# Attention and a Fourier mixer on one TensorE: another order for short matmul steps and pieces of VectorE work

## Chip, cores, metric

One core of one Trainium2 chip. The metric is the device time of one execution in microseconds (us). Times are medians. TensorE is called PE in the profiles, VectorE DVE, ScalarE ACT, GpSimd POOL; SP only issues transfers. L405 is line 405 of the kernel that was profiled, so the same statement has slightly different numbers in the kernel before, the changed kernel and the experiments.

## The reference

Block-sparse attention for four batches and eight heads (768 rows, head width 64) feeds a Fourier mixer with a feed-forward part. Cut to what matters:

```python
# q, k, v: (4, 8, 768, 64) float32; mask: blocks of 32, window, border blocks, three random ones
scores = np.where(mask, scale * q @ k.T, -1e9)
attn = softmax(scores) @ v                         # (4, 8, 768, 64)
x = attn.transpose(0, 2, 1, 3).reshape(4, 768, 512)

u = x + np.real(fft(fft(x, axis=1), axis=2))       # Fourier mixing
un = (u - mean(u)) / sqrt(var(u) + 1e-6)
out = u + np.maximum(un @ w_ch1, 0) @ w_ch2        # 512 -> 2048 -> 512, weights given as float64
```

The float64 weights come in as 32-bit words and are rounded to float32 on the chip.

## The kernel before

The kernel works through 96 attention steps, 24 to a batch and six to a pair of heads. A step makes two units of scores `s`, their exponentials and the product with the mask `e` (ScalarE, VectorE), and one step later the values `o`. Beside the attention of batch b it works off the mixer of batch b-1. Its front is a chain: divide by the sums and fold the symmetric halves (VectorE, into `sa`, `sd`), the two transforms (`zp`, then `pq`), normalization, turning the result (`utp`). Behind the front stand the channel steps: 32 of `hp` (eight matmuls each) and 24 of `y` (eight each), which need nothing but weights and the turned rows and fill most of the time.

Besides these there are short pieces, three or four small matmuls with a copy behind them: the turn of q and k of the next pair (`tp`), the place of a finished attention output into `x` (`xt`), the total of a pair's sums (`sp`). All of them share one buffer in PSUM, where a matmul's result lies until an engine copies it out: the pool `ps_t`. A piece can start only when the copy of the piece before it has emptied the buffer.

```python
ps_t = ctx.enter_context(tc.tile_pool(name="ps_t", bufs=1, space=PSUM))
...
def turn(n):                                  # q and k of a pair, all in one go
    raw = loaded.pop(n)
    for a, t in enumerate(raw):
        for half in range(2):
            tp = ps_t.tile([P, HS], FP32, tag="t", name="tp")
            for c in range(T):
                nc.tensor.transpose(tp[:, c * P:(c + 1) * P], t[:, T * half + c, :, :], ident)
            if half == 0:
                nc.vector.tensor_copy(out=dst[:, 0:HS], in_=tp)
            else:
                nc.scalar.copy(out=dst[:, HS:S], in_=tp)
        ...
def place(n, half):
    ...
    nc.vector.tensor_copy(out=x_of[b, half][:, :, j * P:(j + 1) * P], in_=xt)
...
def fill():                                   # mixer steps, paid from a budget per attention step
    spent = 0.0
    while early and spent < RATE / 2 and len(late) <= 4 * T:    # front: fold, zp, pq, utp
        cost, fn = early.popleft(); fn(); spent += cost
    ...
    while spent < RATE and late:                                # channel steps
        cost, fn = late.popleft(); fn(); spent += cost

def slot(sl):
    ...values and scores of the step...
    if 0 < sl <= B * SB and sl % (SP // 2) == 0:
        ...
        place(n, half)
    if sl > SB and sl % SP == 0 and sl <= B * SB:
        total(sl // SP - 1)
    if sl >= SB + 2 and (sl - 2) % SB == 0 and (sl - 2) // SB <= B:
        norm(b); queue.append(mixer(b, ...))
    if sl % SP == 3 and sl // SP + 1 < len(pairs):
        turn(n); load_qk(n + 1)
    ...
    fill()
```

The rounding of a weight chunk ends with a product and a sum on GpSimd. The first pair's q and k are loaded on one queue, q first.

Of the kernel before, what the change touches and what calls it, by code (L numbers as in the profile page):

```python
# [82 lines left out]
def kernel(  # L83
# [84 lines left out]
    def load_q(dst, b, h, n):  # L168

        for t in range(C):  # L170
            if t < T:
                for p0, cnt, rows in _rows(q[b, h], t, ((S * D, n),)):
                    nc.sync.dma_start(out=dst[p0:p0 + cnt, t, 0:n, :], in_=rows)
                continue
            for i in range(n):
                for p0, cnt, rows in _rows(q[b, h + i], t):
                    nc.sync.dma_start(out=dst[p0:p0 + cnt, t, i, :], in_=rows)

    def load_qk(n):

        b, j = pairs[n]
        qt = ld.tile([P, C, 2, D], FP32, tag="q", name="qr")
        load_q(qt, b, 2 * j, 2)
        kt = ld.tile([P, C, 2, D], FP32, tag="k", name="kr")
        for i in range(2):
            nc.sync.dma_start(out=kt[:, :, i, :],
                              in_=k[b, 2 * j + i].rearrange("(p c) d -> p c d", p=P))
        loaded[n] = (qt, kt)
# [83 lines left out]
    def mask_step(c):  # L272

        for half in range(2):
            m = ps_m.tile([P, 512], FP32, tag="m", name="m")
            nc.tensor.matmul(m[:, 0:HS], of_k[0:NB, c * P:(c + 1) * P],
                             keep_q[0:NB, half * HS:(half + 1) * HS], start=True, stop=True)
            nc.scalar.copy(out=mask[:, c, half * HS:(half + 1) * HS], in_=m[:, 0:HS])
# [59 lines left out]
    for w, w_sb in ((w_ch1, w1_sb), (w_ch2, w2_sb)):  # L338
        rows, cols = w.shape
        words = _words(w, rows * cols)  # L340
        for col in range(0, cols, WN):
            for row in range(rows // P):
                src = bass.AP(tensor=words, offset=2 * (row * P * cols + col),
                              ap=[[2 * cols, P], [1, 2 * WN]])
                wchunks.append((src, w_sb[:, row, col:col + WN]))
# [12 lines left out]
    def w_load(i):  # L358

        n1 = len(wchunks) // 2  # L360
        t = room(2 + i % 4 if i < n1 else 4 + i % 2, [P, 3 * WN], "wraw", U32)
# [3 lines left out]
    def w_round(i):  # L365
# [16 lines left out]
        nc.gpsimd.tensor_mul(out=a.bitcast(FP32), in0=lo.bitcast(FP32), in1=a.bitcast(FP32))  # L382
        nc.gpsimd.tensor_add(out=dst, in0=dst, in1=a.bitcast(FP32))
# [8 lines left out]
    def turn(n):  # L392

        raw = loaded.pop(n)
        out2 = []
        for a, t in enumerate(raw):
            dst = tp_p.tile([P, S], FP32, tag="qk"[a] + "T", name="qk"[a] + "T")
            for half in range(2):
                tp = ps_t.tile([P, HS], FP32, tag="t", name="tp")
                for c in range(T):  # L400
                    nc.tensor.transpose(tp[:, c * P:(c + 1) * P],  # L401
                                        t[:, T * half + c, :, :], ident)
                if half == 0:
                    nc.vector.tensor_copy(out=dst[:, 0:HS], in_=tp)  # L404
                else:  # L405
                    nc.scalar.copy(out=dst[:, HS:S], in_=tp)
# [3 lines left out]
            out2.append(dst)  # L410
        turned[n] = out2
# [5 lines left out]
    def scores(u):  # L417
        n, w = divmod(u, UP)
        half, c = divmod(w, C)
        qT, kT = turned[n]  # L420
# [30 lines left out]
    def values(u):  # L451
# [10 lines left out]
        if c == C - 1:  # L462
            if half == 1:
                v_of.pop(n)
                turned.pop(n)
# [4 lines left out]
    def place(n, half):  # L470
# [5 lines left out]
        xt = ps_t.tile([P, T, P], FP32, tag="t", name="xt")  # L476
        for c in range(T):
            nc.tensor.transpose(xt[:, c, :], oT[:, c * P:(c + 1) * P], ident)
        nc.vector.tensor_copy(out=x_of[b, half][:, :, j * P:(j + 1) * P], in_=xt)  # L479
# [40 lines left out]
    def norm(b):  # L520

        r = sm.tile([P, T, 4, NP], FP32, tag="r", name="r", bufs=2)
        for half in range(2 if b == 0 else 1):
# [5 lines left out]
            if b > 0:  # L529
                nc.vector.reciprocal(out=r, in_=st[:, :, :, 0:NP])  # L530
                continue
# [4 lines left out]
        if b == 0:  # L536
            nc.vector.reciprocal(out=r, in_=r)
        for half in range(2):
            for c in range(T):
                xc = x_of[b, half][:, c, :].rearrange("p (j i d) -> p j i d", i=2, d=D)  # L540
                rc = r[:, c, 2 * half:2 * half + 2, :].rearrange("p i (j o) -> p j i o", o=1)
                nc.vector.tensor_tensor(out=xc, in0=xc, in1=rc.broadcast_to([P, NP, 2, D]),  # L542
                                        op=ALU.mult)
# [6 lines left out]
    def fourier(b, xA, xB, uns):  # L550
# [3 lines left out]
        def fold():  # L554
            sa = next_room([P, T, DM], "sa")
            sd = next_room([P, T, DM], "sd")
            e1 = un_p.tile([P, DM], FP32, tag="un", name="e1")
            tt = nc.vector.tensor_tensor
            tt(out=sa, in0=xA, in1=xB, op=ALU.add)
            tt(out=sd, in0=xA, in1=xB, op=ALU.subtract)  # L560
            tt(out=sa[:, :, 1:M], in0=sa[:, :, 1:M], in1=_run2(sa, DM - 1, M - 1, -1), op=ALU.add)
            tt(out=sd[:, :, 1:M], in0=sd[:, :, 1:M], in1=_run2(sd, DM - 1, M - 1, -1),
               op=ALU.subtract)

            b1 = xB[:, 1, :]
# [4 lines left out]
            top = slice(DM - QD, DM)  # L570
            for f in (sa, e1.rearrange("p (o d) -> p o d", o=1)):
                tt(out=f[:, :, top], in0=f[:, :, 0:QD], in1=_run2(f, M, QD, -1), op=ALU.add)  # L572
                tt(out=f[:, :, 0:QD], in0=f[:, :, 0:QD], in1=_run2(f, M, QD, -1),
                   op=ALU.subtract)

            tt(out=sd[:, :, top], in0=sd[:, :, 0:QD], in1=_run2(sd, M, QD, -1), op=ALU.subtract)
            tt(out=sd[:, :, 1:QD], in0=sd[:, :, 1:QD], in1=_run2(sd, M - 1, QD - 1, -1),
               op=ALU.add)
            nc.vector.tensor_copy(out=sd[:, :, 0:1], in_=sd[:, :, QD:QD + 1])
            st["f"] = (sa, sd, e1)  # L580
            st["z"] = tr_p.tile([P, 4, KS], FP32, tag="tr", name="z")
            st["side"] = sm.tile([1, KS], FP32, tag="side", name="side", bufs=1)
# [3 lines left out]
        def along(g):  # L586

            sa, sd, e1 = st["f"]
            ps = ps_m.tile([P, 512], FP32, tag="m", name="zp")
# [28 lines left out]
        def across(m):  # L618
# [18 lines left out]
            tt = nc.vector.tensor_tensor  # L637
# [36 lines left out]

        steps = [(0.0, fold)]
        steps += [(2.0, lambda g=g: along(g)) for g in range(5)]
        for m in range(T):
            def both(m=m):
                across(m)
                whiten(0, m)  # L680
            steps.append((1.2, both))
        return steps, whiten
# [3 lines left out]
    def mixer(b, xA, xB):  # L686

        uns, unT = {}, {}
        first, whiten = fourier(b, xA, xB, uns)
# [12 lines left out]
        def hidden(half, f):  # L702
            if f % 4 == 0:
                if b == half == f == 0:

                    turns[0] = ROOMS
# [30 lines left out]
        first += [(0.6, lambda m=m: un_flip(0, m)) for m in range(T)]  # L737
        rest = []
        for half in range(2):
            for f in range(NF):  # L740
                rest.append((2.6, lambda half=half, f=f: hidden(half, f)))
                if half == 0 and f in (2, 4, 6):
                    rest.append((0.0, lambda m=f // 2 - 1: whiten(1, m)))
                if half == 0 and f in (5, 7, 9):
                    rest.append((0.6, lambda m=(f - 5) // 2: un_flip(1, m)))
            for m in range(T):
                for part in range(4):
                    rest.append((3.5, lambda half=half, m=m, p=part: channels(half, m, p)))
        return first, rest

    def run_all(steps):
        for _, fn in steps:
            fn()
# [3 lines left out]
    RATE = 5.6  # L757
    W_PACE = 0.9
    SP = UP // SLOT
    SB = SP * NP  # L760
    early, late, queue = deque(), deque(), deque()
    w_next = w_got = 0

    def fill():


        if not early and queue and queue[0][0]:
            early.extend(queue[0][0])
            queue[0][0].clear()
        spent = 0.0  # L770
        while early and spent < RATE / 2 and len(late) <= 4 * T:
            cost, fn = early.popleft()
            fn()
            spent += cost
        if not early and queue and not queue[0][0]:
            late.extend(queue.popleft()[1])
        while spent < RATE and late:
            cost, fn = late.popleft()
            fn()
            spent += cost  # L780

    def slot(sl):
        nonlocal w_next
        units = range(SLOT * sl, SLOT * sl + SLOT)
        if 0 < sl <= B * SB:
# [3 lines left out]
            if sl <= SB:  # L789
# [3 lines left out]
        if sl < B * SB:  # L793
            for u, s in [(u, scores(u)) for u in units]:
                weigh(u, s)
        if 0 < sl <= B * SB and sl % (SP // 2) == 0:
            n, half = divmod(sl // (SP // 2) - 1, 2)
            b, j = pairs[n]
            while j == 0 and b >= 2 and (b - 2, half) not in finished:
                late.popleft()[1]()  # L800
            place(n, half)
        if sl > SB and sl % SP == 0 and sl <= B * SB:
            total(sl // SP - 1)
        if sl >= SB + 2 and (sl - 2) % SB == 0 and (sl - 2) // SB <= B:
            b = (sl - 2) // SB - 1
            norm(b)
            queue.append(mixer(b, x_of.pop((b, 0)), x_of.pop((b, 1))))
# [141 lines left out]
```

## Time and profile before

| kernel before | |
|---|---|
| median of the first three runs | 1451.74 us (1449.76 to 1460.52) |
| span of the profiled run | 1454.3 us |
| PE busy, PE idle | 1224.2 us, 230.1 us |
| first scores, first hp | 18.99 us, 275.7 us |

PE is the bound, and its busy time includes the extra that a slow clock costs. So I take three numbers from every profile: PE idle (span less busy); PE's excess busy time over 1112 us, the prediction's estimate of the same matmuls at full clock; and whatever PE's view of waits names. The prediction shows the main lines.

```profile
618.23 7.94 DMA out_dram<-x
```

The copy that places attention output into `x` waits twice for an output transfer that still reads that buffer, for two batches earlier. Such a transfer takes 8 us. PE's two longest waits of `sp` for `x` in the prediction's list, 9.36 and 9.20 us of its 42.4, are this; the prediction overlooked it.

### The profile page before, as it was taken

Reading aid. Unit: us, or ns where it says so; the run is one execution under the profiler, and the core shown is the slowest. Engines: PE = TensorE matmul, PEld = TensorE weight load, DVE = VectorE, ACT = ScalarE, POOL = GpSimd, SP = SyncE. Lnnn points to the kernel's source line nnn. Section 1 sums busy time; section 2 is a strip of 40 time slices with the busy share of each in tenths; the row PEclk is TensorE's granted clock in tenths of the full one; section 3 lists DMA queues with packets and bytes.
Section 4 is the critical chain, followed back from the end, with each engine's and each line's share of the span. In section 5 each row is a group of like instructions: output and inputs, shape, how many; then the busy total and the mean of one; then the engine's idle time right before and its main releaser. Section 6 shows DMA issues by size and latency. Waiting matters only on the chain.

```text
span 1454.3 us, 11918 instructions
## 1 busy us (share of the span) xinstructions
PE 1224.2 (84%) x4412; PEld 574.2 (39%) x4412; DVE 426.2 (29%) x817; ACT 310.0 (21%) x541; POOL 321.6 (22%) x245
## 2 busy tenths in 40 slices
PE   5888748789898968868989895878999996899996
PEld 1222214344334423434434442334444443454552
DVE  2335184443122252413212225322221223320000
ACT  3455324232112112113112211202212110010000
POOL 1225253344222221112222221202222220000000
PEclk9899878799999989889999998889999998999998
DMA  4433321111010100000010000000100000000000
GB/s 117 114 110 99 91 69 51 40 32 45 17 38 8 26 7 22 8 18 22 11 37 19 22 11 8 22 25 1 33 8 8 8 1 8 8 7 8 15 2 23
DMA packets 65281, 44.26 MB, mean 30 GB/s; under 512 B 52902, under 2 KB 58048, under 8 KB 65216
## 3 DMA queue, kind: packets, MB, share of 16 engines
q1 hardware_dynamic: 65216, 43.42, 10.8%
q8 instruction: 37, 0.61, 0.2%
q14 instruction: 28, 0.23, 0.1%
HBM read 37.11 MB, written 6.29 MB: 30 GB/s over the span
## 4 chain that ended last, share of the span: by engine, by line
PE 67%; DVE 7%; ACT 2%; DMA 1%; issue 1%; DVEq 0%; ACTq 0%
PE y L725 24%; PE hp L710 23%; PE o L460 6%; PE s L423 6%; PE tp L401 2%; DVE e L443 2%; PE zp L596 1%; DMA out_dram<-x 1%; DVE x L542 1%; ACT s L441 1%; PE utp L697 1%; PE zp L607 1%; PE sp L516 1%; DVE x L479 1%; DVE kT L404 0%
## 5 line engine op out<-in xcount | busy, mean ns | idle before, releaser
L710 PE MATMUL hp<-unT,w_sb 128*128 128x384 f32 x1024 | 358.9, 508 | 2.0 <-ACT unT L698 2.0
L725 PE MATMUL y<-w_sb,hs 128*128 128x512 f32 x768 | 351.0, 612 | 0.0
L449 POOL TENSOR_TENSOR acc<-acc,e 128x768 f32<-128x768 f32 x96 | 175.2, 1825 | 404.1 <-DVE e L443 400.3
L710 PEld LDWEIGHTS hp<-unT,w_sb 128*128 128x128 f32 x1024 | 199.4, 199 | 150.9 <-issue 31.4
L443 DVE TENSOR_TENSOR e<-s,mask 128x768 f32<-128x768 f32 x144 | 131.1, 952 | 339.3 <-ACT s L441 339.3
L725 PEld LDWEIGHTS y<-w_sb,hs 128*128 128x128 f32 x768 | 148.5, 197 | 186.0 <-issue 182.8
L460 PE MATMUL o<-e,vr 128*64 128x384 f32 x768 | 159.0, 532 | 11.2 <-ACT e L439 8.4
L441 ACT ACTIVATE s<-s 128x768 f32<-128x768 f32 x144 | 108.0, 792 | 243.8 <-PE s L423 243.8
L423 PE MATMUL s<-qT,kT 64*128 64x384 f32 x768 | 159.6, 524 | 0.0
L716 DVE TENSOR_SCALAR hs<-hp 128x384 f32<-128x384 f32 x64 | 35.6, 557 | 220.7 <-PE hp L710 220.7
L423 PEld LDWEIGHTS s<-qT,kT 64*128 64x128 f32 x768 | 65.3, 189 | 84.8 <-issue 66.4
L714 ACT ACTIVATE hs<-hp 128x384 f32<-128x384 f32 x64 | 31.4, 491 | 314.0 <-PE hp L710 314.0
L447 POOL TENSOR_TENSOR acc<-e 128x768 f32<-128x768 f32 x24 | 43.3, 1806 | 228.7 <-PE sp L516 124.8
L460 PEld LDWEIGHTS o<-e,vr 128*64 128x64 f32 x768 | 47.7, 142 | 109.1 <-issue 82.7
L382 POOL TENSOR_TENSOR wraw<-wraw 128x512 f32<-128x512 f32 x32 | 41.5, 1297 | 192.4 <-issue 73.0
L596 PE MATMUL zp<-cs_sb,sa 128*128 128x385 f32 (+1 forms) x48 | 27.4, 712 | 53.4 <-DVE sa L572 53.4
L401 PE MATMUL tp<-ident,qr 128*128 128x128 f32 x96 | 24.8, 335 | 51.4 <-DVE x L479 28.7
L730 DVE TENSOR_TENSOR x<-y,x 128x512 f32<-128x512 f32 x24 | 16.6, 691 | 159.9 <-PE y L725 159.9
L439 ACT ACTIVATE e<-s 128x768 f32<-128x768 f32 x48 | 38.8, 811 | 55.1 <-PE s L428 55.1
L516 PE MATMUL sp<-acc,pick 128*32 128x384 f32 x96 | 13.1, 618 | 42.4 <-DVE x L479 42.4
L401 PE MATMUL tp<-ident,kr 128*128 128x128 f32 x96 | 27.6, 422 | 19.9 <-DVE kT L404 10.4
L375 DVE TENSOR_SCALAR wraw<-wraw 128x512 uint32<-128x512 uint32 x32 | 16.4, 512 | 93.8 <-ACT wraw L374 93.7
(139 smaller groups left out, 719.8 us busy)
## 6 DMA issues: line engine op xcount, KB each, us to landing
wraw<-in_moe_w_ch_dram SPq DMA_DIRECT2D x32, 512.0 KB
kr<-in_k_dram SPq DMA_DIRECT2D x32, 192.0 KB
vr<-in_v_dram SPq DMA_DIRECT2D x32, 192.0 KB
qr<-in_q_dram SPq DMA_DIRECT2D x128, 32.0 KB
out_dram<-x SPq DMA_DIRECT2D x16, 128.0 KB
out_dram<-x SPq DMA_DIRECT2D x8, 256.0 KB
qr<-in_q_dram SPq DMA_DIRECT2D x64, 31.5 KB
qr<-in_q_dram SPq DMA_DIRECT2D x64, 0.2 KB
```

What stands on the lines that cost most here:

```text
L382: nc.gpsimd.tensor_mul(out=a.bitcast(FP32), in0=lo.bitcast(FP32), in1=a.bitcast(FP32))
L401: nc.tensor.transpose(tp[:, c * P:(c + 1) * P], t[:, T * half + c, :, :], ident)
L423: nc.tensor.matmul(s[:, i, 0:HS], kT[D * i:D * i + D, c * P:(c + 1) * P], qT[D * i:D * i + D, half * HS:(half + 1) * HS], start=True, stop ...
L439: nc.scalar.activation(out=e, in_=s[:, :, 0:HS], func=ACT.Exp, scale=scale)
L441: nc.scalar.activation(out=s[:, :, 0:HS], in_=s[:, :, 0:HS], func=ACT.Exp, scale=scale)
L443: nc.vector.tensor_tensor(out=e, in0=s[:, :, 0:HS], in1=m.broadcast_to([P, 2, HS]), op=ALU.mult)
L447: nc.gpsimd.tensor_add(out=acc_of[n, half], in0=e_of[u - 1], in1=e)
L449: nc.gpsimd.tensor_add(out=acc_of[n, half], in0=acc_of[n, half], in1=e)
L460: nc.tensor.matmul(o[D * i:D * i + D, :], vt[:, i, c, :], e[:, i, :], start=(c == 0), stop=(c == C - 1))
L596: mm(ps[rows, 0:KS], sa[:, t, cols], cs_sb[:, t, :], start=(t == 0), stop=False)
L710: nc.tensor.matmul(ps[:, 0:T * P], w1_sb[:, d, f * P:(f + 1) * P], unT[half][:, d, :], start=(d == 0), stop=(d == ND - 1))
L725: nc.tensor.matmul(y, hs[half, f // 4][:, f % 4, m * P:(m + 1) * P], w2_sb[:, f, :], start=(f == 0), stop=(f == NF - 1))
```

## The change

Intent: put every short piece behind a channel step, one at a time, so that PE has long matmuls to run while the piece's copy empties the shared buffer; cut VectorE's long front work into eight folds and six scalings that go between channel steps as well; and keep channel steps of the last batch back (28, then 12) for the front of the next. With that go several smaller edits. The diff, cut to its core:

```diff
-    def turn(n):                       # four tp groups, one behind the other
+    def turn(n, a, half):              # one tp group; four calls per pair
+        pool, tag = small(pairs[max(n - 1, 0)][0])      # batch 0: ps_m (two buffers), else ps_t
...
-                if half == 0:
-                    nc.vector.tensor_copy(out=dst[:, 0:HS], in_=tp)
-                else:
-                    nc.scalar.copy(out=dst[:, HS:S], in_=tp)
+        if a == 0:
+            nc.vector.tensor_copy(out=dst[:, half * HS:(half + 1) * HS], in_=tp[:, 0:HS])
+        else:
+            nc.scalar.copy(out=dst[:, half * HS:(half + 1) * HS], in_=tp[:, 0:HS])
...  place:
-        nc.vector.tensor_copy(out=x_of[b, half][:, :, j * P:(j + 1) * P], in_=xt)
+        nc.scalar.copy(out=x_of[b, half][:, :, j * P:(j + 1) * P],
+                       in_=xt[:, 0:HS].rearrange("p (c f) -> p c f", c=T))
...  w_round:
-        nc.gpsimd.tensor_mul(out=a.bitcast(FP32), in0=lo.bitcast(FP32), in1=a.bitcast(FP32))
-        nc.gpsimd.tensor_add(out=dst, in0=dst, in1=a.bitcast(FP32))
+        nc.vector.tensor_mul(out=a.bitcast(FP32), in0=lo.bitcast(FP32), in1=a.bitcast(FP32))
+        nc.vector.tensor_add(out=dst, in0=dst, in1=a.bitcast(FP32))
...  load_qk:
+        second = nc.scalar if n == 0 else nc.sync       # first k and half of first q: ScalarE's queue
...
+    RATE = 2.4                          # channel steps per attention step
+    def gap():                          # behind every channel step
+        if short:
+            short.popleft()()           # one short piece, or
+            return
+        room_for = 2                    # up to two pieces of VectorE work or one group of front matmuls
+        while apart and room_for > 0:
+            kind, fn, need = apart[0]
+            if kind == "p" and room_for < 2:
+                return
+            while len(late) > need:     # need: channel steps kept back
+                channel_step()
+            apart.popleft()
+            ...
+    def begin(b):
+        hold = 4 * T
+        wide = hold + NF
+        steps = [(kind, fn, wide) for kind, fn in norm_steps(b) + first]
...  slot:
+            for at, a, half in ((1, 0, 0), (2, 0, 1), (4, 1, 0), (5, 1, 1)):
+                if s == at:
+                    short.append(lambda a=a, half=half: turn(n + 1, a, half))
...
+        state["owed"] = min(state["owed"] + RATE, RATE + 1) if late else 0.0
+        gap()
+        while late and state["owed"] >= 1:
+            channel_step()
+            state["owed"] -= 1
+            gap()
+        while short:
+            gap()
```

Also: six buffers for weight chunks in place of four and then two, 1.3 chunks per attention step in place of 0.9, and the chunks in another order; two mask matmuls per attention step as short pieces; the loads of q and k for a later pair at step 5 in place of 3; and the second half of a batch's first pair is placed two attention steps later.

## The prediction

> **What bounds the kernel now.** I read the page first: busy time by engine, then the 40 slices.
>
> ```profile
> PE 1224.2 (84%) x4412; PEld 574.2 (39%) x4412; DVE 426.2 (29%) x817; ACT 310.0 (21%) x541; POOL 321.6 (22%) x245
> ...
> PE   5888748789898968868989895878999996899996
> ...
> PEclk9899878799999989889999998889999998999998
> ```
>
> TensorE is the bound, 84% busy; nothing else passes 29%. The slices where PE falls to 4 to 6 are those where the clock falls to 7 or 8. They come about every 350 us: at the start of each batch's Fourier mixer. PE is idle for 1454 - 1224 = 230 us. The view of waits, PE alone, says why:
>
> ```profile
> PE zp L596 <- DVE sa L572: 53.4, 4, 14.5
> PE sp L516 <- DVE x L479: 42.4, 12, 9.4
> PE tp L401 <- DVE x L479: 28.7, 15, 3.4
> PE pq L614 <- DVE x L657: 13.7, 3, 4.6
> PE tp L401 <- DMA qr<-in_q_dram: 13.0, 6, 4.4
> ```
>
> All waits of PE in that view sum to 218 us; the other 12 are the output at the end. The three largest, 124 us, are of one kind: a short matmul stands in PE's order directly behind the VectorE piece or the PSUM buffer that it needs, with long matmuls behind it that could have run. The timeline of PE inside an otherwise full stage shows one:
>
> ```profile
> 700.03 0.55 PE L478 MATMUL xt<-ident,oT 128*128 128x128 f32 x3
> 702.83 0.85 PE L516 MATMUL sp<-acc,pick 128*32 128x384 f32 x8 [2.25 <-DVE x L479]
> 703.61 5.43 PE L710 MATMUL hp<-unT,w_sb 128*128 128x384 f32 x16
> ```
>
> sp needs the one buffer that xt filled; its copy waits in VectorE's queue behind two mask products (952 ns each). PE stands for 2.25 us with two hp steps ready behind it.
>
> **The floor.** I take each kind of matmul where the timeline shows it back to back at granted clock 1.00. Channel steps: the last stage has 128 hp in 41.28 us and 96 y in 41.20 us, so 322 and 429 ns; 1024 x 0.322 + 768 x 0.429 = 660 us. Attention: a step of two units takes 697.10 to 700.03 = 2.93 us for o and s; 96 of them 281. The first batch also has the mask as a matmul and its sums: 0.74 + 0.78 a step, x24 = 36. Short groups tp and xt: 96 groups of three x 0.48 = 46. Later sums 12 x 0.78 = 9, mask 3. The Fourier part (zp, pq, end, utp, st) by its start-to-start intervals is about 19 a batch, 76. Sum: **1112 us**. Busy time is 1224, so 112 us are the slow clock; idle 230. 1112 + 112 + 230 = 1454.
>
> **What the Trainium skill says.** "TensorE: Matmul & The Clock Gate", "HAM oscillation": the clock is full only while PE stays busy, and gaps longer than some 3.4 us put it to half. The trace agrees in kind and is harsher: after gaps of only 2 us, eight hp matmuls took 4.36 us instead of 2.58. The same page, Part 2: matmuls stay in program order, only weight loads are pulled ahead; so the place in PE's order decides, as the 2.25 us show. "Perfetto Trace Analysis", "Matmuls": independent groups should rotate through PSUM banks so that one's evacuation overlaps the next one's matmuls; xt, tp, sp share one buffer here, and the waits above are its price. "SBUF — State Buffer", "Who interferes with whom": VectorE reading two SBUF inputs contends with GpSimd. Agrees: the rounding's scalar_tensor_tensor took 0.69 us alone and 1.66 us beside GpSimd's product.
>
> **The change part by part.**
>
> 1. *One short piece behind each channel step.* No matmul is added or removed; the order on each engine changes, and I compared both orders. In the new one tp, xt, sp and st stand alone between hp or y steps of 2.58 or 3.43 us, which is longer than an evacuation (0.56 us) even behind two mask products (1.82). The fold and scaling (before: some 14 us of VectorE in one run, with PE waiting) are cut into pieces and, for batches 1 to 3, stand behind channel steps kept back for that. So sp<-x (42.4), tp<-x (28.7), tp<-qT/kT (28) and about 40 of the 53.4 us for zp should go: about 139 us.
>
> 2. *No filler for batch 0.* The first batch has no channel steps, and the new order has up to three gaps of short work per attention step instead. There the first hp comes three attention steps later than before. VectorE work in this stage: ten steps x 1.82 = 18, scaling 5, fold 12, pq and normalization 16, copies 4 = 55 us; PE's own work is about 29 + 19 + 5 = 53. With the chains s, exp, product, o in each step, I estimate 78 us, of them 25 idle. Before, the stretch from 187 to 276 us took 89 with fewer attention steps.
>
> 3. *Ends of the later fronts.* In batches 1 and 2 the order runs out of channel steps at pq; the last pq and the utp behind it stand with only attention steps of 2.93 us between. A pq piece is some 4.5 us of VectorE plus 2.4 of normalization. I keep 6 to 7 us idle a batch, 20 in all.
>
> 4. *q and k in four parts, first loads on two queues.* The six tp groups wait for qr 4.4, 1.4, 1.3, 2.0, 2.1, 1.9 us, since 18 q loads take 11 us to issue one after the other. k and half of q go to ScalarE's queue, which is idle then: first scores at about 14 us instead of 19.
>
> 5. *Rounding on VectorE alone, all six buffers, pace 1.3.* Removed: 64 GpSimd operations of 1.30 us, none of which PE waited for. Added to VectorE: 64 x about 0.59 (a 1536-wide fp32 sum takes 1.76) = 38 us. A chunk is then 0.46 + 0.72 + 0.40 + 1.18 = 2.76 us; at 1.3 a step 3.6 of the 4.84 us that a step of batch 0 takes. With tables and copies about 85% of VectorE: it fits. ScalarE: 1.62 of exp, 1.46 of rounding, 0.8 of copies = 3.9 of 4.84. Weights finish at step 25 instead of 36, and the deeper prefetch should remove the one stall of 6.7 us where o waited for an exp behind a late chunk. The mask matmuls come two a step with one free buffer: about 12 us idle where 4.7 were.
>
> **The sum.** Idle left: start 10, batch 0 20, first front 25, later fronts 20, scattered 15 (a pq holds one of the two channel buffers), output 12 = 102 us. Slow clock: before, 112 us for 230 idle, 0.49 each; 0.49 x 102 = 50. 1112 + 102 + 50 = **1264 us**, a ratio of 0.87.
>
> **Rivals.** (a) *VectorE takes over as the wait.* Its queue is first in, first out; two pieces behind one step (up to 3.5 us) plus the two products delay o and the copies that free PSUM. For: the first front holds 55 us of VectorE work in 78. Against: 29% busy overall, and o has waited only 11 us for e. If it bites in every front and in batch 0, +50: 1310. (b) *Transfers bound batch 0.* 16.8 MB of weights, 5.9 of q, k, v and 1.4 of tables in about 130 us is 186 GB/s; the most that a 30 us window moved is 156 GB/s at a busy share of 0.53, so room seems left, but packets of q are small and ScalarE's queue stops exp behind a late chunk. Worth +15 to +30. (c) *The clock stays full.* If gaps become too short to trip the gate, slow clock goes to 15 or less: 1220. (d) *Nothing moves,* because waits only shift to the next matmul in order. Against: the channel steps were runnable when PE stood idle, and no engine is near full; I give this little.
>
> **Range and chances.** (c) with small leftovers gives 1210, (a) and (b) together 1325. Even half of the recovered idle leaves about 1360, below the 2% line at 1423. Predicted 1264, 1210 to 1325; faster by over 2%: 0.96, within 2%: 0.03, slower: 0.01.
>
> **What would show it.** Right: sp<-x and tp<-x gone from PE's waits, zp's wait at most one long item (batch 0), mean granted clock near 0.95 to 0.96, PE busy near 1160 in a span of 1264, first hp before 240 us, all slices from the tenth on at 9 apart from one per batch. Wrong: o waiting for VectorE's e over 40 us in total (rival a), exp or rounding waiting for weight transfers over 15 us (rival b), the clock still at 0.91, or hp and y waiting for their own evacuations, which they never did before.

## More of the kernel before

One more pair belongs here, from the view of DVE's waits and from the chain of waits of the kernel before (columns of the first: us in total, times, longest; of the second: start, duration, what):

```profile
DVE x L479 <- DMA out_dram<-x: 16.4, 2, 8.3
```

## The result and the profile after

| | before | after |
|---|---|---|
| median of four runs | 1456.13 us (1449.76 to 1460.78) | 1262.11 us (1260.93 to 1263.47) |
| ratio to before, 95% interval | | 0.867 (0.8627 to 0.8714) |
| span of the profile | 1454.3 us | 1261.3 us |
| PE busy, less 1112 | 112 us | 41 us |
| PE idle | 230 us | 108 us |
| first scores, first hp | 18.99, 275.7 us | 25.40, 277.6 us |

Ratios are the mean time of one kernel's fast runs over that of the other's fast runs of the same rounds, so not quite the ratio of the medians quoted.

The page of the changed kernel, busy time and the 40 slices:

```profile
PE 1153.3 (91%) x4412; PEld 546.8 (43%) x4412; DVE 446.3 (35%) x849; ACT 320.8 (25%) x573; POOL 239.9 (19%) x181
...
PE   3859796879999999969999999969999999999996
...
PEclk9889897889999999979999999979999999999998
```

From the tenth slice on every digit is 9 but for one per batch. The number of matmuls, 4412, is unchanged. The stretch table shows where the rest of the idle time lies (stretch, its length, then busy us of PE, PEld, DVE, ACT and POOL with numbers of instructions, granted clock, DMA share, GB/s):

```profile
0.00:30.00 30.00, 8.52 (x28) 3.51 (x28) 7.41 (x40) 5.37 (x9) 1.90 (x13) 1.00 0.52 158
30.00:180.00 150.00, 122.26 (x679) 39.95 (x677) 87.40 (x190) 83.85 (x144) 0.00 (x0) 0.89 0.43 130
180.00:300.00 120.00, 95.83 (x438) 45.73 (x435) 78.44 (x148) 45.89 (x84) 41.95 (x32) 0.89 0.10 24
300.00:540.00 240.00, 240.00 (x898) 114.40 (x897) 81.54 (x126) 55.81 (x100) 63.55 (x39) 1.00 0.09 24
540.00:570.00 30.00, 19.26 (x81) 10.97 (x80) 9.67 (x23) 8.30 (x15) 7.52 (x6) 0.77 0.03 9
```

The 240 us from 300 on have no idle time at all, at full clock. Idle time is 21.5 us in the first 30, 27.7 in the next 150, 24.2 in the first front to 300, and 10.7 in one hole at 540; a second hole, 10.6 us with the short gaps behind it, is at 825 to 845, and the end takes 12. PE's view of waits now reads:

```profile
PE tp L405 <- DMA qr<-in_q_dram: 24.1, 9, 7.7
PE tp L405 <- ACT x L481: 19.1, 3, 9.2
PE m L277 <- DVE qT L407: 10.2, 2, 9.5
PE o L462 <- DVE e L445: 10.0, 4, 6.4
PE tp L405 <- DVE qT L407: 6.5, 1, 6.5
```

The lines `zp` for `sa` and `sp` for `x`, 96 us of the kernel before, are gone, though 18.6 us of the second, the output transfer, come back as `tp` for `x`. What leads now was small or absent: transfers. Three of these lines end in one even where they name an engine. The timeline shows it (start, duration, engine, line, operation; in brackets the engine's idle time just before and what ended it):

```profile
80.72 0.75 DVE L292 COPY cs_sb<-tab 128x128 f32<-128x128 f32 x7 [10.61 <-DMA tab<-in_cos_s_dram]
```

```profile
84.96 0.47 PE L277 MATMUL m<-at_q,at_k 24*128 24x384 bf16 x1 [9.55 <-DVE qT L407]
```

VectorE stood 10.61 us at the copy of a Fourier table that had not arrived; the copy of `qT`, which frees the PSUM buffer that PE's mask matmul needs, stood behind it in the same queue. VectorE stood at tables before the change too (11.3, 5.3 and 1.3 us), but PE hardly felt it: it was busy 29.3 of the 30 us around the longest of these waits (90 to 120). New is that copies which turn parts and mask matmuls wait for now stand right behind the table copies. And at 540:

```profile
540.95 7.98 DMA out_dram<-x
```

```profile
549.18 0.48 ACT L481 COPY x<-xt 128x384 f32<-128x384 f32 x1 [11.72 <-DMA out_dram<-x]
549.72 0.98 PE L405 MATMUL tp<-ident,qr 128*128 128x128 f32 x3 [9.19 <-ACT x L481]
```

The copy into `x` waits for the 8 us output transfer, as before the change. But it now stands directly in front of a turn part that wants the same PSUM buffer, and no channel step is left to run.

### The profile page after: what moved, and what is told of

It is laid out like the page before. It is cut to its first block, busy times and chain, and to the rows that moved or that the text cites. A ratio compares the mean times of both kernels' runs of the same rounds, so it can differ in the third digit from the quotient of the medians.

```text
span 1261.3 us, 11815 instructions
## 1 busy us (share of the span) xinstructions
PE 1153.3 (91%) x4412; PEld 546.8 (43%) x4412; DVE 446.3 (35%) x849; ACT 320.8 (25%) x573; POOL 239.9 (19%) x181
## 4 chain that ended last, share of the span: by engine, by line
PE 84%; DMA 4%; SPq 4%; DVE 4%; ACT 2%; issue 1%; POOL 0%; ACTq 0%; DVEq 0%
PE hp L726 26%; PE y L741 26%; PE o L462 10%; PE s L425 10%; PE tp L405 2%; DMA qr<-in_q_dram 2%; SPq L177 2%; SPq L173 2%; DMA out_dram<-x 1%; PE zp L616 1%; PE zp L627 1%; PE utp L716 1%; PE sp L506 1%; PE xt L480 1%; DMA wraw<-in_moe_w_ch_dram 1%
## 5 line engine op out<-in xcount | busy, mean ns | idle before, releaser
L726 PE MATMUL hp<-unT,w_sb 128*128 128x384 f32 x1024 | 340.6, 487 | 0.7 <-ACT unT L717 0.7
L741 PE MATMUL y<-w_sb,hs 128*128 128x512 f32 x768 | 338.7, 594 | 0.0
L726 PEld LDWEIGHTS hp<-unT,w_sb 128*128 128x128 f32 x1024 | 190.2, 190 | 126.8 <-issue 5.3
L741 PEld LDWEIGHTS y<-w_sb,hs 128*128 128x128 f32 x768 | 142.8, 190 | 168.9 <-issue 166.5
L425 PE MATMUL s<-qT,kT 64*128 64x384 f32 x768 | 163.1, 534 | 0.0
L405 PE MATMUL tp<-ident,qr 128*128 128x128 f32 x96 | 21.8, 319 | 50.7 <-DMA qr<-in_q_dram 24.1
L685 POOL TENSOR_SCALAR rstd<-mv 128x1 f32<-128x1 f32 x24 | 5.3, 219 | 194.0 <-DVE mv L683 193.5
L405 PEld LDWEIGHTS tp<-ident,qr 128*128 128x128 f32 x96 | 11.4, 147 | 66.8 <-issue 31.9
L468 ACT COPY oT<-o 128x384 f32<-128x384 f32 x32 | 15.2, 476 | 82.9 <-PE o L462 82.9
L407 DVE COPY qT<-tp 128x384 f32<-128x384 f32 x32 | 17.6, 551 | 47.7 <-PE tp L405 47.7
```

The lines of the kernel that those rows point to most:

```text
L425: nc.tensor.matmul(s[:, i, 0:HS], kT[D * i:D * i + D, c * P:(c + 1) * P], qT[D * i:D * i + D, half * HS:(half + 1) * HS], start=True, stop ...
L726: nc.tensor.matmul(ps[:, 0:T * P], w1_sb[:, d, f * P:(f + 1) * P], unT[half][:, d, :], start=(d == 0), stop=(d == ND - 1))
L741: nc.tensor.matmul(y, hs[half, f // 4][:, f % 4, m * P:(m + 1) * P], w2_sb[:, f, :], start=(f == 0), stop=(f == NF - 1))
```

## The experiments

All times of a table's row are of one chip session with the kernel before, whose median was 1455.3 to 1456.4 us in all of them, so the differences from 1262.1 can be compared across sessions. "Idle" and "slow clock" are of the profiled run: span less PE busy, and PE busy less 1112.

| run | median, us | ratio to before (95%) | from 1262.1 | idle | slow clock |
|---|---|---|---|---|---|
| changed kernel | 1262.1 | 0.867 (0.863 to 0.871) | | 108 | 41 |
| e1 loads on one queue | 1244.1 | 0.854 (0.853 to 0.855) | -18 | 91 | 43 |
| e2 weights behind q | 1253.4 | 0.860 (0.859 to 0.862) | -9 | 99 | 41 |
| e3 rounding on GpSimd | 1258.7 | 0.864 (0.862 to 0.867) | -3 | 106 | 40 |
| e4 turn whole | 1306.6 | 0.898 (0.896 to 0.900) | +44 | 125 | 63 |
| e5 fold in one run | 1258.3 | 0.864 (0.862 to 0.866) | -4 | 107 | 39 |
| e6 no steps kept back | 1314.8 | 0.903 (0.901 to 0.905) | +53 | 140 | 61 |
| e7 short pieces together | 1270.2 | 0.872 (0.870 to 0.874) | +8 | 114 | 41 |
| e8 output in columns | 1262.0 | 0.866 (0.864 to 0.868) | 0 | 102 | 43 |
| e9 two tables in flight | 1249.4 | 0.858 (0.856 to 0.859) | -13 | 98 | 38 |
| e14 four parts undone | 1374.5 | 0.944 (0.942 to 0.946) | +112 | 179 | 82 |
| e10 loads, tables, output | 1227.6 | 0.845 (0.842 to 0.848) | -34 | 77 | 36 |
| e15 e10 with fold in one run | 1228.3 | 0.844 (0.842 to 0.846) | -34 | 81 | 32 |

Every run gave correct results. Repeats of one version lie within some 8 us (of the kernel before, 11); differences of 4 us and less I take for nothing.

### Parts of the change undone

**e4: the turn in one piece.**

```diff
-            for at, a, half in ((1, 0, 0), (2, 0, 1), (4, 1, 0), (5, 1, 1)):
-                if s == at:
-                    short.append(lambda a=a, half=half: turn(n + 1, a, half))
+            if s == 4:
+                short.append(lambda: [turn(n + 1, a, half) for a in range(2) for half in range(2)])
```

> The four parts of a pair's turn stay one piece, as before the change, put behind one channel step; all else as in the changed kernel. Theory (each part is a round trip between TensorE and a copying engine through one PSUM buffer, and only cutting it lets other TensorE work lie between): three waits of about 0.65 us or more for each of 16 pairs, plus the clock that those pauses cost, 35 to 50 us longer, near 1300. Rival (the later channel steps and the scores fill these pauses anyway): within 10 us of 1262.

Measured: +44 us. PE's waits:

```profile
PE tp L405 <- DVE qT L407: 41.1, 30, 3.6
...
PE tp L405 <- ACT kT L409: 10.1, 16, 1.5
```

The theory holds, and its size in total. 46 waits at one buffer come back, 51 us where the changed kernel has 8. Idle time rises by only 17, because the shifted order happens to lose the waits for `x` (19.1) and of `m` (10.2); the clock costs 21 more. (The profiled run was 5 us under the median.) Cutting the turn is one of the two parts of the change that pay.

The waits are not all the 0.65 us round trips of the theory. From batch 1 on the first of a turn is mostly 2.1 to 2.2 us. PE's timeline of e4, then that of the kernel before:

```profile
654.86 0.74 PE L405 MATMUL tp<-ident,qr 128*128 128x128 f32 x3 [2.16 <-DVE qT L407]
```

```profile
738.03 0.67 PE L401 MATMUL tp<-ident,qr 128*128 128x128 f32 x3 [2.16 <-DVE x L479]
```

In both, the first VectorE copy of the group stands behind two mask products (1.82 us together: in e4 from 652.51, the copy of `qT` at 654.25). Before the change that copy was the one of `x`, since place and turn shared an attention step. So e4 brings back, under another name, most of what the kernel before lost at `tp` for `x` and for the turn's own copies, 28.7 + 28.0 = 56.7 us.

**e6: no channel steps kept back.**

```diff
-        hold = 4 * T
-        wide = hold + NF
+        hold = 0
+        wide = 0
```

> No channel steps are kept back for the next batch's front; the pieces are still cut and put one behind each step. Theory (the fronts of the later batches are hidden by the 28 and 12 channel steps kept back for them): fronts of batches 1 and 2 are then as exposed as the first one's (about 24 us idle each), the last one's, without attention beside it, about 45, with the clock some 80 us longer, near 1340. Rival (the attention beside the front hides it whatever the order): 0 to 15 us longer.

Measured: +53 us. The theory's direction holds against the rival; its 80 was too much. Idle rises by 32 and the clock costs 20. `zp` waits for `sa` again:

```profile
PE zp L616 <- DVE sa L589: 22.3, 3, 11.2
```

**e5: scaling and fold in one run.**

```diff
-        steps = [(kind, fn, wide) for kind, fn in norm_steps(b) + first]
+        parts = norm_steps(b) + first
+        scaled = [fn for kind, fn in parts if kind == "d"]
+        steps = [... the st group ...]
+        steps.append(("d", lambda: [fn() for fn in scaled], wide))
+        steps += [... zp groups ...]
```

> Scaling and folding of a batch run on VectorE in one piece again, at one place; channel steps are still kept back for the front. Theory (keeping channel steps back already covers most of it; what stays is that the mask products, values and hidden steps behind the run of about 14 us wait for VectorE): about 20 us longer, near 1282. Rival (the cutting itself is what hides the front): 40 to 50 us longer, over 1300.

Measured: -4 us, no difference. Both expectations were wrong. The waits show an exchange:

```profile
PE zp L616 <- DVE sa L589: 24.7, 4, 8.5
...
PE tp L405 <- ACT x L481: 3.0, 1, 3.0
```

`zp` waits 24.7 us for the long VectorE run, but the wait for `x` behind the output transfer, 19.1 before, is down to 3.0, presumably since the whole front moved against it. So this run alone does not tell what the cut is worth; e15 below asks again with that wait out of the way.

**e7: short pieces together.**

```diff
         gap()
+        while short:
+            gap()
         while late and state["owed"] >= 1:
```

> All short pieces of an attention step (part of a turn, place, total) are run together, ahead of the step's channel steps, in place of one behind each channel step. Only steps with two short pieces change, that is where a place or total of q and k's pair falls on one step with another piece. Theory (two pieces back to back share one PSUM buffer, each waiting for the other's copy): 10 to 12 places of about 2 us with the clock they cost, 25 to 30 us longer than 1262. Rival (only the split of the turn matters, as run e4 gave 44 us): within 5 us.

Measured: +8 us, with one new line in PE's waits:

```profile
PE sp L519 <- ACT x L481: 8.4, 9, 1.0
```

Nine places where `sp` follows `xt` directly, just under 1 us each and with no cost in clock (41 as before). The theory had 2 us each and the clock on top: right place, a third of the size. I had taken the 2.25 us from the kernel before, where the copy of `x` stood behind mask products on VectorE; on ScalarE it does not.

**e3: rounding on GpSimd again.**

```diff
-        nc.vector.tensor_mul(out=a.bitcast(FP32), in0=lo.bitcast(FP32), in1=a.bitcast(FP32))
-        nc.vector.tensor_add(out=dst, in0=dst, in1=a.bitcast(FP32))
+        nc.gpsimd.tensor_mul(out=a.bitcast(FP32), in0=lo.bitcast(FP32), in1=a.bitcast(FP32))
+        nc.gpsimd.tensor_add(out=dst, in0=dst, in1=a.bitcast(FP32))
```

> The product and the sum of the rounding of the weights go back to GpSimd; everything else as in the changed kernel. Theory (the rounding was beside the path, its move to VectorE is worth little): 0 to 10 us longer than the changed kernel's 1262, about 1262 to 1272. Rival (the rounding's chain across two engines was a main part of the time before): 40 us or more longer, above 1300.

Measured: -3 us, no difference. The groups by form show the exchange, the changed kernel first, then e3 (busy us, mean ns of one):

```profile
L376 DVE SCALAR_TENSOR_TENSOR w_sb<-wraw 128x512 uint32<-128x512 uint32 x32 | 23.6, 739 | 1.1
L381 DVE TENSOR_TENSOR wraw<-wraw 128x512 f32<-128x512 f32 x32 | 22.1, 692 | 1.1
L379 DVE TENSOR_SCALAR wraw<-w_sb 128x512 uint32<-128x512 uint32 x32 | 13.7, 427 | 1.1
```

```profile
L376 DVE SCALAR_TENSOR_TENSOR w_sb<-wraw 128x512 uint32<-128x512 uint32 x32 | 36.2, 1131 | 1.1
L379 DVE TENSOR_SCALAR wraw<-w_sb 128x512 uint32<-128x512 uint32 x32 | 22.2, 694 | 1.1
```

64 operations of 0.69 us, 44 us, leave VectorE, yet its busy time only falls from 446.3 to 434.4: what stays of the rounding gets slower beside GpSimd. Off the path, neither shows in the time.

**e14: all four of e4 to e7 undone at once**, with rates, copy engines, rounding and loads as changed.

> Turn whole, scaling and fold in one run, no channel steps kept back and short pieces together, all at once; rates, copy engines, weight rounding and loads as in the changed kernel. Alone, the first gave +44 us, the second 0, the third +52. Theory (the cut of the VectorE run and the steps kept back are two covers for one thing, so the cut costs nothing alone and much when the other is gone): more than the sum of the single effects, over 1262 + 44 + 52 + 25 = 1383, near 1420. Rival (the parts overlap, the rest of the gain comes from rates, engines of copies and rounding): below 1370.

Measured: +112 us, where the single effects add to 44 - 4 + 53 + 8 = 101. They nearly add. Neither expectation was met: the rival's bound of 1370 was missed by 4.5 us, the theory's of 1383 by 8.5 and its 1420 by 46. PE's waits:

```profile
PE tp L405 <- DVE qT L407: 48.8, 30, 4.8
PE zp L616 <- DVE sa L589: 45.1, 4, 11.6
```

So `zp` is back, and the turn in full: `tp` waits 48.8 + 10.1 = 58.9 us for its copies, against 56.7 before (28.7 of them named after `x`). But `sp` for `x` (42.4 before) is only at the 8.4 us of e7. The kernel before is still 81 us slower than e14, 51 of it idle. What separates them: the copy into `x` is on ScalarE, the turn no longer stands in the same attention step as the place (step 4 of six against step 3), channel steps come at an even 2.4 per attention step, and rounding, loads and buffers. The largest differences in PE's waits are `sp` for `x`, 34 us less (18.6 of the 42.4 were the output transfer, which this order does not run into), and `pq` for `x` on VectorE, 13 less (13.7 to 0.7). For the rest of `sp` the move of the copy to ScalarE is the likely cause: its single waits fall from 2.25 us to about 1. None of these edits was run alone, so this part is argued and not shown.

### New waits of the changed kernel

**e1: the first loads as before the change.**

```diff
-        second = nc.scalar if n == 0 else nc.sync
-        kt = ...; second.dma_start(k...)
-        qt = ...; load_q(qt, b, 2 * j, 2, second)
+        qt = ...; load_q(qt, b, 2 * j, 2)
+        kt = ...; nc.sync.dma_start(k...)
```

> The first pair's q and k are loaded as before the change: one queue, q ahead of k. Theory (the change's two queues delay the first scores from 18.99 to 25.40 us, because the weights' 3 MB go out in front of q's last small packets): first scores at about 19, 6 us earlier, and the run about 6 us shorter, near 1256. Rival (the start costs nothing, since later waits give the 6 us back): same time as the changed kernel within 1 us.

Measured: -18 us, three times the theory's 6.

```profile
18.44 1.65 PE L424 MATMUL s<-qT,kT 64*128 64x384 f32 x4
```

First scores come 7.0 us earlier, as the theory says. The rest, up to the first `hp`: VectorE's waits at the tables fall from 10.6 and 7.6 to 8.6 and 2.2 us, together 7.4, so that the first `hp` comes at 263.1 in place of 277.6. Why the second table's wait shrank this much the run does not tell.

**e2: two queues, but the first six weight chunks behind q.**

```diff
-        nc.sync.dma_start(out=t[:, 0:2 * WN].bitcast(I32), in_=wchunks[i][0])
+        queue_of = nc.scalar if i < ROOMS else nc.sync
+        queue_of.dma_start(out=t[:, 0:2 * WN].bitcast(I32), in_=wchunks[i][0])
```

> Two queues as in the change, but the first six weight chunks (3 MB) are issued behind the first pair's q on the second queue, so that they cannot be ahead of it. Theory (weights crowd out q): last half of q lands well before 21.96 us, first scores at 15 to 19 us, run 6 to 10 us shorter. Rival (the second queue itself is slow: its small packets run on few engines): last half of q still near 22 us, first scores near 25, no gain; the rounding of weights then starts later too.

Measured: -9 us, in the theory's range.

```profile
18.47 1.65 PE L426 MATMUL s<-qT,kT 64*128 64x384 f32 x4 [1.58 <-ACT kT L410]
```

With the same two queues the first scores come at 18.47 too. It was not the second queue that was slow; on the free first queue the weights' 3 MB were issued at 7.99 to 14.6 us and ran beside q's rows.

**e9: tables copied one attention step later.**

```diff
-        if table_put:
-            table_put.pop()()
+        if len(table_put) == 2 or (table_put and not table_steps):
+            table_put.pop(0)()
```

> Each table of the Fourier step is copied one attention step later than in the changed kernel, so that two table transfers are in flight; nothing else moves. Theory (VectorE's queue stood behind the tables' transfers, 10.61 and 7.63 us, and the TensorE waits of 9.55 and 6.52 us behind qT are its echo): both waits go below 1 us, run 12 to 20 us shorter. Rival (the transfers are late because the DMA queue is full of q, k and weights at that time, so a later copy waits as well): waits stay over 4 us and the run is within 4 us.

Measured: -13 us; the theory's range began at 12. The waits behind the tables shrink and do not vanish: VectorE's go from 10.6 and 7.6 to 4.8 and 3.5 us, PE's `m` for `qT` from 10.2 to 4.8, `tp` for `qT` goes from 6.5 to nothing. So both theory and rival have a part: the transfer really is late, one step more covers half of it, and what PE saw was VectorE's queue standing.

**e8: output tiles in four column pieces.**

```diff
-            for p0, cnt, rows in _rows(out[b], T * half + m):
-                nc.sync.dma_start(out=rows, in_=x[p0:p0 + cnt, m, :])
+            for c0 in range(0, DM, DM // 4):
+                for p0, cnt, rows in _rows(out[b][:, c0:c0 + DM // 4], T * half + m):
+                    nc.sync.dma_start(out=rows, in_=x[p0:p0 + cnt, m, c0:c0 + DM // 4])
```

> Each transfer of an output tile is cut into four of 128 columns each; bytes and order are the same. In the changed kernel the transfer of a 256 KB tile with its rows in two runs took about 8 us at a DMA share of 0.13, that is on about 2 of 16 engines. Theory (two engines per transfer, so four transfers go side by side): the copy of x at the start of batches 2 and 3 no longer waits 11.7 us, the turns behind it (9.19 and 9.02 us) wait under 3, the end shrinks by about 6, the run is 12 to 18 us shorter. Rival (all four pieces go to the same two engines): waits and time unchanged or 1 to 3 us worse for the smaller packets.

Measured: no difference. The rival is right: the copy of `x` still stood 11.6 us and the turn behind it 9.1. The stretch of 2 us in the middle of that transfer:

```profile
542.00:544.00 2.00, 0.00 (x0) 0.00 (x0) 0.00 (x0) 0.00 (x0) 0.00 (x0) 0.50 0.14 44
```

The DMA share is 0.14, about 2 of 16 engines, for four pieces together as it was (0.13) for one. The Trainium skill has a rule that fits, "DMA: Bandwidth & Descriptors", "Why a DMA increments its semaphore by 16 and not by 1": a transfer runs on the largest number of engines, up to 16, that divides the slowest dimension of both its access patterns, and from this kind of queue on the lowest-numbered ones. The output's rows are given as two runs of 64, so by this rule every such transfer has two engines, and the same two. The share agrees with two; which two the trace does not show.

### A version with the waits taken out

**e10** joins e1 and e9 and drains the last channel steps of a batch one attention step earlier, so that its last output transfer starts earlier:

```diff
-        if sl < B * SB and n % NP == 1 and s == 2:
+        if sl < B * SB and n % NP == 1 and s == 1:
             b = pairs[n - 1][0]
             while b >= 2 and (b - 2, 1) not in finished:
                 channel_step()
+        if sl < B * SB and n % NP == 1 and s == 2:
             short.append(lambda: place(n - 1, 1))
```

> A version to beat the changed kernel: first pair's loads on one queue, table copies one step later, and the last channel steps of a batch drained one attention step before their x buffer is wanted, so that the 8 us output transfer is over by then. Theory (each removes its own wait): loads 18, tables about 8 of their 12 (the two share one wait), output about 17 idle and 8 clock: near 1212; the turn's waits of 9 us behind the copy of x are gone. Rival (gains overlap, or the drain takes channel steps that the front needs): 1225 to 1245.

Measured: 1227.6 us, 34 less than the changed kernel, ratio 0.845. It beats both kernels, and by less than the theory's 1212; the rival's range holds. PE is busy 94% of the span; its waits:

```profile
PE o L461 <- DVE e L444: 10.4, 3, 6.6
PE utp L715 <- DVE qT L406: 10.2, 3, 6.9
PE tp L404 <- ACT x L480: 5.6, 4, 2.4
```

`tp` behind `x` is down from 19.1 to 5.6 us. But `utp` now waits 10.2 for `qT` (3.7 in the changed kernel), presumably because the drained channel steps are missing behind the front. Most of the gain is from batch 0: VectorE's table waits fall to 0.7 us and the first `hp` comes at 249.3, 28.3 us earlier, so that some 6 to 8 us are left for the output part, to which the theory gave 25.

**e15** is e10 with scaling and fold in one run, as in e5.

> The run e10 with scaling and fold in one VectorE piece. In run e5 that cost nothing, but there 24.7 us of waits of zp for sa appeared while the waits behind the output transfer (19.9 us) shrank to 3.0. Theory (those two cancelled, the cut itself is worth its 25 us): 20 to 30 us longer than e10. Rival (channel steps kept back cover the run, the cut is worth nothing): within 6 us of e10.

Measured: 1228.3 against 1227.6, no difference. The rival is right.

```profile
PE zp L615 <- DVE sa L588: 21.9, 4, 8.5
...
PE o L461 <- DVE e L444: 6.0, 4, 3.1
...
PE tp L404 <- ACT x L480: 2.4, 2, 1.5
```

With the fold in one run `zp` waits 21.9 us, but `o` waits 4.4 less, `tp` behind `x` 3.2 less, `utp` for `qT` 9.3 less (0.9 in place of 10.2; against that, 3.8 for `sums` are new), and PE's busy time is 3.9 less. It looks as if in pieces the same VectorE work delays the short pieces around it instead of the one matmul behind it. The cut into pieces, the most visible part of the change, is worth nothing here, with channel steps kept back; without them it was not tried alone.

## Why the prediction was right or wrong

The time, 1264 predicted and 1262.1 measured, is right, and so are both terms over the floor: 102 us idle (measured 108) and 50 us slow clock (41). The parts of the sum are right in fewer places than their total. The start and batch 0 had 49 us of idle time where 30 were predicted (21.5 + 27.7 against 10 + 20), and the 15 us called scattered hardly came: behind 300 us there are 1.3 outside the two holes and the end. That these two errors nearly cancel is luck.

1. **One short piece behind each channel step; fold in pieces; steps kept back.** Of the waits that were to vanish most did: the `tp` round trips, `zp` for `sa`, and the waits behind mask products; only the output transfer's 18.6 us stayed (19.1, as `tp` for `x`). But the step took three mechanisms as one. Shown to pay: the turn in four parts (44 us, e4) and the channel steps kept back (53 us, e6). Shown not to: the cut of the fold (e5, e15). One piece at a time is worth 8 (e7). Of the 71 us of waits behind the copy of `x`, the 28.7 of `tp` belong to the turn: with the turn whole they come back under the name of `qT` (e4, e14). Of the 42.4 of `sp` only 8.4 come back with the short pieces together (e7, e14), so the rule credited with them is not the main cause there. 18.6 were the output transfer; for the other 15 or so the copy's move to ScalarE, which the prediction did not treat on its own, is the likely cause.
2. **Batch 0.** Predicted 20 us idle in batch 0 and 25 in the first front, first `hp` before 240 us; measured 27.7, 24.2 and 277.6. The front is right. The date failed because batch 0 itself ended late. Of the 37.6 us that it was late, 11.4 are the first scores (25.40 where 14 was predicted) and 16.7 are PE's waits for `qT` behind the table copies (10.2 + 6.5); the other 9 or so are not accounted for. Tables that come late are in kind rival (b), transfers, but the weights that the rival named show no wait near its sign of 15 us (PE's line for `wraw` is 0.9); and VectorE stood as long at tables before the change (17.9 us against 18.2), so what is new is the order behind them.
3. **Ends of the later fronts.** Predicted 20 us, measured 21 in two holes, for another reason. The `pq` chain hardly shows; the holes are the copy of `x` behind the 8 us output transfer (549.18 and 549.72 above). It was in the profile of before, under the waits for `x`, and I read these two waits as mask products. The agreement in size is luck.
4. **First loads on two queues.** Failed, in sign: 14 us predicted for the first scores, 25.40 measured, 18.99 before. The step counted q's issue time and not what the freed queue would do next, which was to send 3 MB of weights (e1, e2). The Trainium skill had the warning, "DMA: Bandwidth & Descriptors", "Issuing engines are not separate DMA queues": transfers from both queues run on the same engines, and a second one saves only issue time. The case agrees: 18.47 us with two queues and the weights out of the way, 18.44 with one.
5. **Rounding on VectorE alone.** Right that it fits and that its place, VectorE alone or with GpSimd, does not show in the time (e3: -3 us). Its operations were taken at 0.59 us and took 0.69.

The slow clock, 0.49 us for each idle us before, is 0.38 in the changed kernel and 0.36 to 0.50 in the twelve experiments. As an estimate of a knock-on cost the rate was somewhat high. The prediction's reading of a gap needs a correction too. Four gaps stand in front of its 4.36 us (2.09, 0.65, 0.57 and 0.65 us within 7 us), not one of 2 us. A single gap can do it, but need not: of the eight waits of `sp` in the kernel before that took 2.25 us, four were followed by about 3.4 us at half clock and four by none.

Rival (a), VectorE as the wait, did not bite: `o` waited 10.0 us for `e`, against 40 named as its sign. Rival (c), a clock that stays full, came true only in the stretches nearly without gaps (300 to 540, 570 to 810 and 870 to 1230 us, all at 1.00): slow clock is 41 us, not 15. Rival (d), waits that only shift, held for the cut of the fold alone (e5, e15). Still open is which edits removed the waits of `sp` and `pq` behind `x`, and with them most of the 81 us between e14 and the kernel before.

## What to carry to other kernels

Cut a chain of short pieces that go through one shared PSUM buffer, give each its own place among long matmuls, and keep some long work back for the serial front of the next stage: these two bought 44 and 53 us, and their effects nearly added. Cutting long work on a helper engine into pieces only moved the waiting here, so measure it by itself. A wait that vanishes from a list may only have changed its name: compare the sum over a buffer's users, not one line. Before a queue is freed or an order tightened, look which transfer goes out next and which copy in an engine's queue waits for a transfer: here such a copy held up everything behind it on its engine, and PE's list named the engine, not the transfer.

## What the Trainium skill lacked or had wrong

- "TensorE: Matmul & The Clock Gate", "HAM oscillation": it gives some 3.4 us as the gap that matters, and a sum for one kernel with gaps of 3 to 5 us. Here gaps of 2.25 us (`sp` before the change) were followed by half clock in four of eight cases. What many small gaps sum to it does not say: in the fourteen profiles here each microsecond of idle PE time cost 0.36 to 0.50 us of slow clock besides (taking 1112 us as the full-clock work).
- "SBUF — State Buffer", "Who interferes with whom": which operations contend is stated, and the runs agree; what it adds up to is not. Moving 44 us of VectorE work to GpSimd freed 12 us of VectorE (446.3 to 434.4), as the remaining scalar_tensor_tensor went from 739 to 1131 ns and tensor_scalar from 427 to 694.
- The order of an engine's queue is stated, but no page that I found draws from it that a copy which waits for a transfer holds the PSUM buffers of unrelated work: 10.61 us of VectorE at a table became 9.55 us of PE at a mask matmul.
- Nothing else was found wrong; the two statements of the DMA page used above agree with e1, e2 and e8.
